# A table of steps that orders all of layer 1 instead of its first quarter

## The chip, the cores and the metric

The kernel runs on one core of one Trainium2 chip. The metric is the device time of one execution in microseconds (us), as the median of several runs. Where the text speaks of a single execution in detail, it is a profiled one: it has its own time, and a span (from its first to its last recorded instruction).

The core's engines are TensorE (PE in the profile; its weight loads are PEld), VectorE (DVE), ScalarE (ACT), GpSimd (POOL) and SyncE (SP), which here only issues transfers (DMA).

## The reference

Three computations follow each other; all numbers are float32.

```python
# 1: linear attention, 4 batches x 8 heads, 768 tokens, head_dim 32, d_state 16
L  = exp(cum[i] - cum[j]) * (i >= j)           # cum = cumsum(log a), in chunks of 32
y  = ((C @ B.T) * L) @ x  +  (C @ state) * exp(cum)
state = exp(sum(la)) * state + sum_j(B_j x_j * exp(cum_end - cum_j))
# 2: layer 1, on 3072 tokens x 256, w_gate and w_val 256 x 1536, w_out 1536 x 256
x1 = (sigmoid(y @ w_gate) * (y @ w_val)) @ w_out
# 3: layer 2, w_in 256 x 2048, w_out 2048 x 256
h  = x1 @ w_in
out = (h * sigmoid(h)) @ w_out
```

## The kernel before

**Tiling.** The kernel cuts attention into 24 chunks of 128 tokens (q = 0 to 23, six for each batch). Layer 1 works on seven blocks of tokens (b = 0 to 6), which hold 2, 2, 4, 4, 4, 4 and 4 chunks, so that a block is 256 or 512 columns wide on TensorE, and on twelve blocks of its weights (f = 0 to 11, 128 columns of w_gate and w_val and 128 rows of w_out each). Layer 2 follows with 16 weight blocks on six blocks of 512 tokens.

**Exactness.** A product of two float32 matrices is made as three products of rounded parts: each operand is split into a high part `hi` (a copy on ScalarE) and a low part `lo` (a subtraction on VectorE), and the function `three` multiplies hi by hi, hi by lo and lo by hi for both halves of 256 input features: six products for one gate tile `g`, value tile `v` or layer-2 tile `h`. Weights pass through `conv` first: ScalarE scales (line 216), VectorE makes two integer passes (218 and 220), GpSimd adds (229), ScalarE copies the high part (232), VectorE subtracts the low part (234). For token blocks 0 and 1 the output product of the first seven weight blocks uses the unsplit w_out; its split for the later blocks is a step of its own, `z`, with the subtraction in line 263.

**A chunk of attention.** Chunk q loads B and C (`b`), x (`x`) and a row of decays (`a`). VectorE's scan makes the decay matrix `L` (379). From chunk 4 on, B and C are split in three bfloat16 parts (`r`, `p`) and transposed by a DMA (`pt`). TensorE makes the scores `cb` in two halves, which share one PSUM tile; VectorE multiplies each half into `L` (429). TensorE then adds up `y` from the transposed, scaled C (`cwT`, 405) times the state (438) and from L times x (eight narrow products with 32 columns of weights, 445), and the state's increment `st` (four narrow products, 461). `yt` splits y into the operand `xT` of layer 1 (500).

**Layer 1.** For each token block and each weight block: `g` (gate, a sigmoid on ScalarE, 594), `v` (value, times the gate on VectorE, 603), `lo` (low part, 613), `o` (output, added into the tile `acc`, 634).

**What sets the order.** The string ORDER lists steps by name and index; a step is a generator, and each mention of it runs it to its next `yield`. Under `tc.manual_schedule()` every engine keeps the order of the list. In the kernel before the list ends inside token block 3's and chunk 17's steps. The rest of layer 1 comes from a loop of Python over `ticks` (one per token block and weight block). It takes the attention steps of the next token block from `slot_steps` at an even rate between the `g`, `v` and `o` of the present one. There only SyncE keeps the order of the program; on the other engines the scheduler of the language places instructions as its own estimate has them ready.

**Layer 2's weights.** They are loaded and converted during layer 1: the first four of sixteen during token block 4, the other twelve during token block 6, once the storage of attention is free (`astack.close()`), with `stg["behind"]` holding their copies behind the last output of block 5. Layer 2 itself is under the scheduler in both kernels.

Of the kernel before, what the change touches and what calls it, by code (L numbers as in the profile page):

```python
# [21 lines left out]
LAG = 2  # L22

NX = 4
# [4 lines left out]
GRP = 3  # L29
RT = 32  # L30
# [8 lines left out]
ct.2 x.3 g.0.0 v.0.0 L.3 a.4 g.0.1 w.2 cb.2.1 g.0.1 S.1 t.3 t.3 ct.2 w.2 t.3 cb.2.1 st.2 w.3 v.0.0 cb.3.0
p.4.0.2 g.0.1 bw.3 st.2 l.6 wr.3 w.3 v.0.1 l.5 w.3 y.2.0 l.4 y.2.0 y.2.1 l.4 S.2 w.3 t.3 cb.3.0 v.0.1 l.5  # L40
yt.2 w.2 v.0.1 l.4 cw.3 cb.3.1 z.0 z.1 cw.4 l.5 w.2 z.2 p.4.1.1 w.3 b.5 o.0.0 p.4.1.0 yt.2 ct.3 x.4 cb.3.1
g.0.2 ct.3 g.0.2 z.2 v.0.2 w.3 y.3.0 L.4 o.0.0 l.7 w.4 l.7 y.3.0 y.3.1 st.3 b.5 yt.3 g.0.2 pt.4.0 wr.4 w.4
bw.4 yt.3 w.4 l.6 g.1.2 v.0.2 l.6 w.3 w.4 x.6 v.0.2 w.5 g.0.3 st.3 l.7 S.3 g.0.3 r.5 g.1.2 w.5 g.1.2 g.1.0
o.0.1 w.4 g.0.3 wr.5 w.5 g.1.0 v.1.0 g.1.1 g.1.0 o.0.1 w.4 o.0.2 l.8 g.1.1 a.6 w.4 g.1.1 v.1.0 w.5 p.5.0.1
v.0.3 v.1.0 o.0.2 w.6 z.1 w.5 g.0.4 o.1.0 wr.6 v.0.3 ct.4 v.0.3 g.0.4 w.6 v.0.4 w.5 l.9 v.1.1 w.6 g.0.4 l.9
v.0.4 o.0.3 ct.4 wr.7 l.8 w.5 st.4 w.6 o.1.0 l.8 v.0.4 w.7 v.1.2 l.9 p.4.1.2 v.1.1 w.6 st.4 pt.4.1 v.1.2
v.1.1 w.7 g.1.4 o.0.3 g.1.4 cw.5 a.5 g.1.4 g.0.5 w.7 p.5.0.0 g.0.5 r.5 o.1.1 l.10 w.6 o.1.1 v.1.2 w.6 w.7
g.1.5 v.0.5 w.8 o.1.2 v.0.5 p.5.1.1 g.1.5 w.8 cb.4.0 ct.5 g.1.5 g.0.5 l.11 w.7 p.5.0.2 w.8 g.1.3 b.7 o.1.2
wr.8 o.0.4 b.6 p.5.1.2 w.7 g.1.3 p.5.1.0 w.8 v.1.3 l.10 wr.9 v.1.3 v.0.5 o.0.4 l.11 cb.4.0 g.1.3 l.10 g.0.7
w.9 v.1.3 pt.5.0 g.0.6 L.5 g.0.7 w.8 g.0.6 y.4.0 b.8 g.0.7 v.0.6 z.6 cb.4.1 b.6 o.0.5 g.0.6 ct.5 v.0.6 wr.10  # L50
w.9 v.0.7 o.1.3 pt.5.1 w.9 v.1.5 o.1.3 o.0.5 w.8 w.9 l.11 v.0.7 v.1.5 x.5 v.0.6 v.1.5 b.7 o.0.6 v.0.7 v.1.4
cb.4.1 v.0.7 v.1.4 a.7 w.10 z.6 g.0.8 r.6 v.1.4 g.1.6 w.10 g.1.6 o.0.6 r.6 p.6.1.1 lo.0.7 g.0.8 w.9 cb.5.0
v.0.8 w.10 o.1.4 g.0.8 g.1.6 v.0.8 o.1.4 p.6.1.0 w.9 wr.11 w.10 g.1.8 g.1.7 cb.5.0 g.1.8 z.4 w.11 o.0.7 o.1.5
v.0.8 g.1.7 v.0.8 v.1.6 p.6.0.0 lo.0.8 y.4.0 y.4.1 w.11 g.1.8 a.8 g.1.7 v.1.6 w.11 w.10 cb.5.1 v.1.7 o.1.5
p.6.1.2 p.6.0.2 w.11 v.1.7 pt.6.1 v.1.8 v.1.7 v.1.6 o.0.7 cb.5.1 v.1.7 v.1.8 o.1.6 lo.1.7 o.0.8 cw.7 w.11
# [24 lines left out]
v.2.11 st.13 y.12.0 v.2.10 y.12.1 a.16 cb.13.0 o.2.8 b.16 v.2.11 g.3.1 b.16 v.2.10 lo.2.11 g.3.0 yt.12  # L80
lo.2.10 p.14.0.0 o.2.9 p.14.1.0 p.14.1.2 st.13 p.14.1.1 g.3.0 pt.14.1 g.3.0 r.15 v.3.0 r.15 v.3.0 g.3.1
pt.14.0 cb.13.0 o.2.9 L.16 v.3.0 g.3.2 g.3.1 x.14 o.2.10 p.15.1.0 a.15 o.2.10 p.15.0.0 lo.3.0 v.3.1 p.15.1.1
cb.13.1 p.15.0.1 cb.13.1 g.3.2 r.16 p.15.0.2 g.3.2 o.2.11 cw.15 yt.12 pt.15.0 cw.14 L.14 o.2.11 o.2.11 g.3.3
g.3.3 cb.14.0 v.3.1 p.16.0.1 bw.14 y.13.0 o.2.11 cb.14.0 b.17 v.3.2 p.15.1.2 b.17 v.3.1 y.13.0 r.16 y.13.1
ct.14 pt.15.1 yt.13 v.3.1 v.3.2 lo.3.1 v.3.3 x.16 v.3.2 g.3.3 v.3.3 p.16.0.2 p.16.0.0 v.3.3 o.3.0 ct.14
cb.14.1 yt.13 p.16.1.1 pt.16.0 S.13 o.3.1 p.16.1.2 v.3.2 cb.14.1 r.17 o.3.0 p.16.1.0 L.15 cw.16 y.14.0 g.3.4
cb.15.0 o.3.1 y.14.0 y.14.1 r.17 st.14 st.14 x.17 lo.3.2 v.3.4 ct.15 pt.16.1 ct.15 cw.17 g.3.4 p.17.0.0 bw.15
g.3.4 cb.15.0 v.3.4 a.17 yt.14 p.17.0.1 S.14 o.3.2 x.15 yt.14 v.3.3 v.3.4 g.3.5 lo.3.3 g.3.5 p.17.1.1 v.3.4
o.3.2 p.17.1.0 lo.3.4 v.3.5 g.3.5 p.17.0.2 p.17.1.2 v.3.5
# [4 lines left out]
def tile_linattn_moe_moe(  # L94
# [115 lines left out]
    def conv(raw, hi, lo, n, whole=None):  # L210
# [20 lines left out]
        with tc.issue_after(stg["behind"]) if "behind" in stg else nullcontext():  # L231
            nc.scalar.copy(hi, f)
# [269 lines left out]
    def slot_steps(s, q0=0, q1=NQ):  # L502
        ok = lambda q: q0 <= q < q1
        st = []
        add = lambda *key: st.append(lambda: do(*key)) if ok(key[1]) else None
        early = s < 9
        if early:
            add("cb", s + 1, 0)
            add("y", s, 0)
            add("cb", s + 1, 1)  # L510
            add("y", s, 1)
        else:

            def joint():
                do("y", s, 0)
                do("y", s, 1)
                if ok(s + 1):
                    do("ct", s + 1)
                    do("st", s + 1)

            if ok(s):
                st.append(joint)
            add("cb", s + 1, 0)
            add("cb", s + 1, 1)
        add("t", s + 2)
        if ok(s + 2):
            st += [lambda: step("r", s + 2), lambda: do("L", s + 2), lambda: do("r", s + 2)]
        add("yt", s)
# [3 lines left out]
        if ok(s + 2):  # L532
            st.append(lambda: (do("bw", s + 2), do("cw", s + 2)))
# [401 lines left out]
```

## Time and profile before

| what | value |
|---|---|
| time, median of 3 runs | 652.7 us (651.78, 652.70, 654.02) |
| the profiled execution | 652.97 us, of which the span is 651.2 us |
| TensorE busy | 633.4 us, 97% of the span |
| VectorE busy | 421.3 us, 65% |
| ScalarE busy | 326.0 us, 50% |
| GpSimd busy | 111.2 us, 17% |
| chain that ended last | PE 91%, DVE 1%, ACT 1% |
| moved by DMA | 51.18 MB, mean 79 GB/s |

An engine is busy while one of its instructions executes. The chain that ended last is followed back from the last instruction to whatever released each step, so its shares say on which engine the end hangs. TensorE's granted clock was 1.00 of its full 2.4 GHz over the whole span.

### The profile page before, as it was taken

How to read it: one execution, taken by the hardware profiler on the slowest of the kernel's cores; microseconds unless marked ns; L12 is line 12 of the kernel's file. 1: busy time of each engine (PE TensorE's matmuls, PEld its weight loads, DVE VectorE, ACT ScalarE, POOL GpSimd, SP SyncE). 2: the span in 40 equal slices, each digit the busy share in tenths (PEclk: the TensorE clock that was granted, in tenths of full speed). 3: DMA queues.
4: the chain of work that ended last, by engine and by line, in shares of the span. 5: the costliest groups of instructions: out<-in, count | busy, mean ns of one | idle time of the engine just before them, and what ended most of it. 6: DMA issues, size and time to landing. Idle time of an engine off the chain costs nothing.

```text
span 651.2 us, 9850 instructions
## 1 busy us (share of the span) xinstructions
PE 633.4 (97%) x3680; PEld 518.4 (80%) x3682; DVE 421.3 (65%) x660; ACT 326.0 (50%) x649; POOL 111.2 (17%) x129
## 2 busy tenths in 40 slices
PE   4989999999999999999999999999999999999997
PEld 1468997777778877877888878888888888888886
DVE  7998898865867677574347775464655645555643
ACT  3777654453536355343255764454554544544533
POOL 4645524121203033220004310000000000000000
PEclk9999999999999999999999999999999999999999
DMA  7999757547646374341003410000000000000001
GB/s 195 243 256 238 151 106 155 116 78 170 128 99 146 74 158 117 55 144 46 0 1 97 130 34 1 1 33 0 1 34 0 18 16 1 33 1 1 33 0 34
DMA packets 140144, 51.18 MB, mean 79 GB/s; under 512 B 119008, under 2 KB 133536, under 8 KB 140096
## 3 DMA queue, kind: packets, MB, share of 16 engines
q1 hardware_dynamic: 139952, 50.41, 32.5%
q8 instruction: 29, 0.48, 0.3%
q14 instruction: 19, 0.16, 0.1%
q10 hardware_dynamic: 144, 0.13, 0.1%
HBM read 36.80 MB, written 3.24 MB: 61 GB/s over the span
## 4 chain that ended last, share of the span: by engine, by line
PE 91%; DVE 1%; ACT 1%; issue 0%; ACTq 0%
PE h L580 20%; PE acc L634 15%; PE v L580 15%; PE g L580 15%; PE o L839 13%; PE o L860 7%; PE y L445 2%; PE cb L426 2%; PE y L438 1%; PE st L461 1%; DVE w L234 0%; PE cwT L405 0%; PE o L848 0%; ACT st L361 0%; DVE cvt L220 0%
## 5 line engine op out<-in xcount | busy, mean ns | idle before, releaser
L580 PE MATMUL g<-xT,w 128*128 128x512 f32 (+1 forms) x504 | 122.3, 370 | 3.3 <-DVE xT L500 1.2
L580 PE MATMUL v<-xT,w 128*128 128x512 f32 (+1 forms) x504 | 121.2, 369 | 0.0
L580 PE MATMUL h<-x2T,w2b 128*128 128x512 f32 x432 | 107.0, 389 | 0.0
L814 DVE TENSOR_TENSOR sh<-h,sh 128x512 f32<-128x512 f32 x96 | 66.2, 691 | 61.5 <-ACT sh L813 60.0
L823 DVE TENSOR_TENSOR gl<-sh,gh 128x512 fp32r<-128x512 f32 x96 | 65.8, 690 | 57.2 <-ACT gh L818 55.8
L580 PEld LDWEIGHTS g<-xT,w 128*128 128x128 f32 x504 | 86.5, 188 | 19.7 <-DVE xT L500 1.6
L580 PEld LDWEIGHTS v<-xT,w 128*128 128x128 f32 x504 | 86.3, 189 | 14.8 <-issue 1.0
L634 PE MATMUL acc<-gh,w 128*128 128x512 f32 (+1 forms) x280 | 97.3, 382 | 0.2 <-ACT x1T L645 0.2
L580 PEld LDWEIGHTS h<-x2T,w2b 128*128 128x128 f32 x432 | 80.7, 188 | 16.5
L813 ACT ACTIVATE sh<-h 128x512 f32<-128x512 f32 x96 | 57.5, 599 | 71.3 <-PE h L580 67.3
L818 ACT CAST gh<-sh 128x512 fp32r<-128x512 f32 x96 | 59.0, 620 | 61.7 <-DVE sh L814 31.1
L572 ACT CAST gh<-sg 128x512 fp32r<-128x512 f32 (+1 forms) x70 | 41.1, 589 | 75.2 <-DVE sg L603 68.7
L603 DVE TENSOR_TENSOR sg<-v,sg 128x512 f32<-128x512 f32 (+1 forms) x84 | 50.8, 609 | 39.0 <-PE v L580 36.7
L839 PE MATMUL o<-w2b,gh 128*128 128x512 f32 x280 | 74.2, 390 | 0.0
L613 DVE TENSOR_TENSOR gl<-sg,gh 128x512 fp32r<-128x512 f32 (+1 forms) x70 | 47.8, 683 | 27.4 <-ACT gh L572 27.0
L594 ACT ACTIVATE sg<-g 128x512 f32<-128x512 f32 (+1 forms) x84 | 44.8, 537 | 34.9 <-PE g L580 30.9
L229 POOL TENSOR_TENSOR cvt<-cvt,raw 128x512 int32<-128x512 int32 (+1 forms) x28 | 44.5, 1592 | 101.8 <-DVE cvt L220 80.2
L634 PEld LDWEIGHTS acc<-gh,w 128*128 128x128 f32 x280 | 52.4, 188 | 10.4 <-ACT x1T L645 0.6
L839 PEld LDWEIGHTS o<-w2b,gh 128*128 128x128 f32 x280 | 51.8, 188 | 10.3
L379 DVE TENSOR_TENSOR_SCAN L<-L,eye 128x1024 f32<-128x1024 f32 x24 | 55.2, 2300 | 6.0 <-DMA L<-ac_d 6.0
L634 PE MATMUL acc<-gl,w 128*128 128x512 f32 (+1 forms) x140 | 52.6, 376 | 0.0
L429 DVE TENSOR_TENSOR L<-cb,L 128x512 f32<-128x512 f32 x48 | 32.7, 682 | 9.3 <-PE cb L426 7.5
(95 smaller groups left out, 730.3 us busy)
## 6 DMA issues: line engine op xcount, KB each, us to landing
L<-ac_d SPq DMA_DIRECT2D x23, 512.0 KB, 4.6
raw<-in_moe_w_out_dram SPq DMA_DIRECT2D x28, 256.0 KB, 3.3
raw<-in_moe_w_in_dram SPq DMA_DIRECT2D x16, 256.0 KB, 2.7
raw<-in_moe_w_gate_dram SPq DMA_DIRECT2D x12, 256.0 KB, 4.6
raw<-in_moe_w_val_dram SPq DMA_DIRECT2D x12, 256.0 KB, 4.8
x<-in_x_dram SPq DMA_DIRECT2D x24, 128.0 KB, 2.9
out_dram<-o2t SPq DMA_DIRECT2D x20, 128.0 KB, 1.7
bc<-in_B_dram SPq DMA_DIRECT2D x24, 64.0 KB, 3.6
```

The source lines that it names most:

```text
L379: nc.vector.tensor_tensor_scan(t["Lf"], t["Lf"], eye, 0.0, op0=ALU.mult, op1=ALU.add)
L580: nc.tensor.matmul(psum[:, :n], w[:, i, o + k * P : o + (k + 1) * P], xt[j][:, k, :n], start=(z == 0), stop=(z == len(k_terms) - 1),)
L594: nc.scalar.activation(sg[:, :n], ps[:, :n], AF.Sigmoid)
L603: nc.vector.tensor_mul(sg[:, :n], ps[:, :n], sg[:, :n])
L613: nc.vector.tensor_sub(lo[:, :n], sg[:, :n], hi[:, :n].bitcast(F32))
L634: mm = nc.tensor.matmul(o, v[:, ms], g[:, :n], start=(f == 0 and z == 0 and not (small and m)), stop=(f == NF1 - 1 and z == len(terms) - 1 ...
L813: nc.scalar.activation(sg, ps, AF.Sigmoid)
L814: nc.vector.tensor_mul(sg, ps, sg)
L818: nc.scalar.copy(hi, sg)
L823: nc.vector.tensor_sub(lo, sg, hi.bitcast(F32))
L839: nc.tensor.matmul(ps, hi[:, s], w2(f)[:, :, DM:], start=(f == 0), stop=False, skip_group_check=True,)
L860: nc.tensor.matmul(ps[:, :DM], g2[b, f][2][:, s], w2(f)[:, 0, DM:], start=False, stop=(f == NF2 - 1), skip_group_check=True,)
```

## The change

The string ORDER grows from 1015 entries to 1808 and now lists every step of layer 1, of attention and of the loading and conversion of layer 2's weights, so that all engines keep its order up to the last token block of layer 1; its first part is written anew as well. The loop over ticks, `slot_steps`, and the rule that held the conversions behind a copy are gone. Two new entries, `A` and `B`, open the two tiles for layer 2's weights, and `l2`, `w2`, `wr2` load and convert one block of them. Each engine issues the same operations on the same shapes as before; only their order differs.

```diff
-from contextlib import ExitStack, nullcontext
+from contextlib import ExitStack
...
 ORDER = """
-e.0 e.0 b.0 b.0 a.0 e.1 e.1 e.1 e.2 e.1 l.0 l.0 l.0 b.1 e.2 t.0 L.0 x.0 t.0 e.2 L.0 L.0 e.3 t.0 b.1 cb.0.0
...
+l2.15 o.6.8 v.6.9 g.6.11 lo.6.9 v.6.10 w2.13 v.6.10 g.6.11 w2.14 o.6.9 w2.14 w2.15 v.6.11 wr2.14 w2.15 o.6.9
+w2.15 wr2.15 w2.14 v.6.11 g.6.11 w2.15 w2.14 v.6.10 w2.14 w2.15 lo.6.10 v.6.11 w2.15 v.6.11
 """
...
-        with tc.issue_after(stg["behind"]) if "behind" in stg else nullcontext():
-            nc.scalar.copy(hi, f)
+        nc.scalar.copy(hi, f)
...
+    def w2_load(f):
+        return load_w(("w2", f), w2(f), f, (w2_in,), w2_out)
+
+    def w2_conv(f):
+        return conv(*pend["w2", f])
+
+    def w2_conv_r(f):
+        conv_r(pend["w2", f][0])
+
+    def open_a():
+        sstack.close()
+        w2_alloc("a", NA)
+        stg["n"], stg["raw"], stg["cvt"] = 512, 2, 2
+        stg["p"] = sstack.enter_context(tc.tile_pool(name="stg2", bufs=1))
+
+    def open_b():
+        astack.close()
+        w2_alloc("b", NF2 - NA)
+
     FN = dict(
+        A=open_a, B=open_b, l2=w2_load, w2=w2_conv, wr2=w2_conv_r,
...
-    sp_order = ExitStack()
-    sp_order.enter_context(tc.manual_schedule(engines={mybir.EngineType.SP}))
-    ends = [sum(BLOCKS[: b + 1]) for b in range(len(BLOCKS))]
...
-        run(rate)
-        do("g", b, f)
-        run(rate)
-        if prev is not None:
-            do("lo", *prev)
-        do("v", b, f)
-        prev = (b, f)
-        run(rate)
-        queue_o.append((b, f))
-        if len(queue_o) > LAG:
-            do("o", *queue_o.pop(0))
...
-    for o in queue_o[:-1]:
-        do("o", *o)
-    do("lo", *prev)
-    do("o", *queue_o[-1])
+    last = len(BLOCKS) - 1
+    do("o", last, NF1 - 2)
+    do("lo", last, NF1 - 1)
+    do("o", last, NF1 - 1)
```

Three places show how the instructions move. The first is TensorE at chunk 15, in the fourth token block (b = 3). In the rows, `g3_5` is the gate tile of token block 3 and weight block 5, `st15` the state's increment of chunk 15, `cb15_1` the second half of its scores; a number behind the last underscore tells buffers apart, and the line is that of the kernel that the row belongs to. Before:

```order
L634 MATMUL acc3_2168<-gh3_2_2190,w1_105 128x512
L634 MATMUL acc3_2168<-gl3_2_2191,w1_105 128x512
L634 MATMUL acc3_2168<-gh3_2_2190,w1_105 128x512
L461 MATMUL st15_2318<-x15_2271,bw15_2254 32x64
L580 MATMUL v3_5_2296<-xT0_3_1616,w1_105 128x512
L580 MATMUL v3_5_2296<-xT1_3_1617,w1_105 128x512
L580 MATMUL v3_5_2296<-xT0_3_1616,w1_105 128x512 x2
L580 MATMUL v3_5_2296<-xT1_3_1617,w1_105 128x512
L580 MATMUL v3_5_2296<-xT0_3_1616,w1_105 128x512
L461 MATMUL st15_2318<-x15_2271,bw15_2254 32x64 x3
```

The same place in the changed kernel:

```order
L469 MATMUL cb15_0_2306<-tr115_2122,tr015_2137 128x128
L481 MATMUL y14_2311<-cwT14_2040,S13_2120 128x128 x2
L504 MATMUL st15_2315<-x15_2233,bw15_2249 32x64 x4
L488 MATMUL y14_2311<-L14_1930,x14_2054 32x128 x8
L469 LDWEIGHTS tr015_2137
L469 MATMUL cb15_1_2338<-tr115_2122,tr015_2137 128x128
```

Before, the four products of `st15` stood apart, with a value tile between the first and the rest; now all four stand next to the eight narrow products of `y14`, and the two halves of chunk 15's scores stand directly around that group.

The second place is VectorE at the conversion of the first weights. `cvt6`, `cvt8` and `cvt13` are the conversion buffers of weight blocks 2, 3 and 4 before; `w1<-x1T` is the subtraction of step `z`; `L3` and `L4` are the decay matrices of chunks 3 and 4. Before:

```order
L263 TENSOR_TENSOR w1_105<-x1T_81,w1_105 128x256
L234 TENSOR_TENSOR w1_105<-cvt6_249,w1_105 128x512
L500 TENSOR_TENSOR xT1_1_433<-y2_406,xT0_1_432 128x2x128
L429 TENSOR_TENSOR L3_270<-cb3_1_440,L3_270 128x512
L263 TENSOR_TENSOR w1_105<-x1T_81,w1_105 128x256
L379 SCALAR_TENSOR_TENSOR L4_346<-L4_346,eye_97 128x1024
L218 TENSOR_SCALAR cvt13_485<-cvt13_485 128x768
L500 TENSOR_TENSOR xT1_1_433<-y3_478,xT0_1_432 128x2x128
L220 SCALAR_TENSOR_TENSOR cvt13_485<-raw11_409,cvt13_485 128x768
L234 TENSOR_TENSOR w1_105<-cvt8_384,w1_105 128x512
```

In the changed kernel `cvt9` and `cvt12` are the buffers of weight blocks 3 and 4:

```order
L472 TENSOR_TENSOR L3_244<-cb3_0_426,L3_244 128x512
L543 TENSOR_TENSOR xT1_1_444<-y2_407,xT0_1_443 128x2x128
L262 TENSOR_SCALAR cvt12_435<-cvt12_435 128x768
L264 SCALAR_TENSOR_TENSOR cvt12_435<-raw8_346,cvt12_435 128x768
L277 TENSOR_TENSOR w1_105<-cvt9_356,w1_105 128x512
L472 TENSOR_TENSOR L3_244<-cb3_1_468,L3_244 128x512
L422 SCALAR_TENSOR_TENSOR L4_361<-L4_361,eye_97 128x1024
L604 TENSOR_TENSOR sg0_2_479<-v0_2_454,sg0_2_479 128x256
```

The two subtractions of `z` have left this place, and weight block 3's low part (`cvt9`) now stands ahead of chunk 4's scan, where before its counterpart (`cvt8`) stood behind it.

The third place is SyncE's queue at the start. `bc0` holds chunk 0's B and C, `x1T<-in_a` is the load of `a` for the decays, `L0` its broadcast for chunk 0, `raw1` the first weight block. Before:

```order
L665 DMA x1T_81<-in_a_dram 32x768
L308 DMA bc0_117<-in_B_dram 128x8x16
L310 DMA bc0_117<-in_C_dram 128x8x16
L297 DMA L0_120<-in_a_dram 128x8x128
L673 DMA ac_d_108<-x1T_81 32x6x128
L247 DMA raw1_127<-in_moe_w_gate_dram 128x2x256
L247 DMA raw1_127<-in_moe_w_val_dram 128x2x256
```

In the changed kernel:

```order
L351 DMA bc0_115<-in_B_dram 128x8x16
L353 DMA bc0_115<-in_C_dram 128x8x16
L664 DMA x1T_81<-in_a_dram 32x768
L290 DMA raw1_120<-in_moe_w_gate_dram 128x2x256
L340 DMA L0_122<-in_a_dram 128x8x128
L290 DMA raw1_120<-in_moe_w_val_dram 128x2x256
```

B and C of chunk 0 are now ahead of `a`, the first weights ahead of chunk 0's broadcast, and the store of the clipped decays (`ac_d`) has moved behind the second weight block's first load.

## Rows read from the trace of the kernel before

**Rows 1.** Busy time by stretch: us, PE, PEld, DVE, ACT, POOL, PEclk, DMA share, GB/s.

```profile
30.00:50.00 20.00, 17.03 (x140) 13.12 (x140) 19.16 (x29) 15.05 (x35) 11.66 (x13) 1.00 0.96 253
50.00:66.00 16.00, 14.61 (x113) 13.25 (x112) 13.86 (x21) 11.55 (x23) 8.10 (x7) 1.00 0.97 237
...
100.00:320.00 220.00, 219.80 (x1382) 172.54 (x1381) 148.02 (x235) 100.59 (x211) 46.44 (x63) 1.00 0.49 108
```

**Rows 2.** Timeline of TensorE: start, us, operation, [idle before <-releaser].

```profile
38.07 0.74 PE L580 MATMUL g<-xT,w 128*128 128x256 f32 x4 [0.73 <-DVE w L234]
```

**Rows 3.** The chain that ended last, in layer 2: twelve products of 512 columns.

```profile
412.06 2.72 PE h L580 x12
```

**Rows 4.** Timeline of TensorE, a `y` group alone.

```profile
93.15 0.28 PE L634 MATMUL acc<-gl,w 128*128 128x256 f32 x1
93.27 0.28 PE L634 MATMUL acc<-gh,w 128*128 128x256 f32 x1
93.47 0.64 PE L445 MATMUL y<-L,x 128*32 128x128 f32 x16
94.05 0.62 PE L580 MATMUL g<-xT,w 128*128 128x256 f32 x3
94.51 0.40 PE L426 MATMUL cb<-tr,tr 128*128 128x128 bf16 x4
```

**Rows 5.** Timeline of TensorE, an `st` group alone.

```profile
259.94 0.39 PE L634 MATMUL acc<-gl,w 128*128 128x512 f32 x1
260.26 0.32 PE L461 MATMUL st<-x,bw 128*32 128x64 f32 x8
260.51 0.50 PE L634 MATMUL acc<-gh,w 128*128 128x512 f32 x1
260.85 1.56 PE L580 MATMUL g<-xT,w 128*128 128x512 f32 x6
```

**Rows 6.** Timeline of TensorE, both narrow groups side by side.

```profile
110.33 1.07 PE L580 MATMUL g<-xT,w 128*128 128x512 f32 x4
111.33 0.32 PE L461 MATMUL st<-x,bw 128*32 128x64 f32 x8
111.47 0.62 PE L445 MATMUL y<-L,x 128*32 128x128 f32 x16
112.02 0.38 PE L634 MATMUL acc<-gh,w 128*128 128x256 f32 x1
112.24 0.28 PE L634 MATMUL acc<-gl,w 128*128 128x256 f32 x1
```

**Rows 7.** Timeline of VectorE in the first 60 us.

```profile
11.75 0.56 DVE L218 TENSOR_SCALAR cvt<-cvt 128x768 int32<-128x768 int32 x1 [1.29 <-ACT cvt L216]
...
15.37 0.69 DVE L429 TENSOR_TENSOR L<-cb,L 128x512 f32<-128x512 f32 x1 [0.72 <-PE cb L418]
...
38.87 0.41 DVE L263 TENSOR_TENSOR w<-x1T,w 128x256 fp32r<-128x256 f32 x1
39.20 2.28 DVE L379 TENSOR_TENSOR_SCAN L<-L,eye 128x1024 f32<-128x1024 f32 x1
...
47.69 0.69 DVE L234 TENSOR_TENSOR w<-cvt,w 128x512 fp32r<-128x512 f32 x1
...
56.69 2.29 DVE L234 TENSOR_TENSOR w<-cvt,w 128x512 fp32r<-128x512 f32 x1 [0.22 <-ACT w L232]
```

**Rows 8.** Timeline of SyncE's queue, chunk 0's load of B.

```profile
1.26 0.41 SPq L308 DMA_DIRECT2D bc<-in_B_dram  x1
```

**Rows 9.** Timelines of TensorE and VectorE, the second half of a chunk's scores.

```profile
96.28 0.40 PE L426 MATMUL cb<-tr,tr 128*128 128x128 bf16 x4
96.48 0.95 PE L580 MATMUL g<-xT,w 128*128 128x256 f32 x6
...
96.71 0.69 DVE L429 TENSOR_TENSOR L<-cb,L 128x512 f32<-128x512 f32 x1 [0.43 <-PE cb L426]
```

**Rows 10.** Timeline of GpSimd.

```profile
56.57 1.85 POOL L229 TENSOR_TENSOR cvt<-cvt,raw 128x768 int32<-128x768 int32 x1
```

More of the change, by code (lines that the diff above doesn't have):

```diff
@@ L39 @@
[L39 to L43, printed above, removed]
@@ L500, in at_yT @@
         nc.vector.tensor_sub(lo, t["y"], hi.bitcast(F32))
[L502 to L528, printed above, removed]
-        if ok(s + 2) and s + 2 >= NX:
-            for i in range(2):
-                st.append(lambda i=i: ([do("p", s + 2, i, j) for j in range(3)], do("pt", s + 2, i)))
-        if ok(s + 2):
-            st.append(lambda: (do("bw", s + 2), do("cw", s + 2)))
-        if early or not ok(s):
-            add("ct", s + 1)
-            add("st", s + 1)
-        add("S", s + 1)
-        if s >= 1 and ok(s + 3):
-            st.append(lambda: (do("b", s + 3), do("x", s + 3)))
-            add("a", s + 3)
-        return st
     live = {}
@@ L564, in tile_linattn_moe_moe @@
     acc = {}
-    x1_end = []
     g1 = {}
@@ L644, in m1_out @@
                 o = a_[:, m * n : (m + 1) * n] if small else a_[:, m, :n]
-                x1_end[:] = [nc.scalar.copy(x1T[0][:, m, start_of[b] : start_of[b] + n], o)]
+                nc.scalar.copy(x1T[0][:, m, start_of[b] : start_of[b] + n], o)
     scr = lambda k, i: x1T[0][:U, k, i * S : (i + 1) * S]
-    NB0 = BLOCKS[0]
-    slots = lambda s0, s1, q0, q1: [f for s in range(s0, s1) for f in slot_steps(s, q0, q1)]
     first = scr(1, 3)
@@ L705, in tile_linattn_moe_moe @@
             step(name, *map(int, at))
-    sp_order = ExitStack()
-    sp_order.enter_context(tc.manual_schedule(engines={mybir.EngineType.SP}))
-    ends = [sum(BLOCKS[: b + 1]) for b in range(len(BLOCKS))]
-    GR = [range(g, min(g + GRP, NF1)) for g in range(0, NF1, GRP)]
-    ticks = [(b, f) for b in range(2, len(BLOCKS)) for f in range(NF1)]
-    steps = [g for s in range(ends[1], ends[2]) for g in slot_steps(s)]
-    w2st = {}
-    def run(k):
-        for _ in range(min(k, len(steps))):
-            steps.pop(0)()
@@ L720, in tile_linattn_moe_moe @@
-    NA = 4
-    w2 = lambda f: w2st["a"][:, f] if f < NA else w2st["b"][:, f - NA]
-    def w2_alloc(key, n):
-        stack, side = (ctx, "left") if key == "a" else (w1stack, "right")
-        w2p = stack.enter_context(tc.tile_pool(name=f"w2{key}", bufs=1, side=side))
-        w2st[key] = w2p.tile([P, n, 2, 2 * DM], F32R, name=f"w2{key}")
-    def w2_steps(f0, f1):
-        ld = lambda f: lambda: walk(load_w(f, w2(f), f, (w2_in,), w2_out))
-        cv = lambda f: lambda: (conv_r(pend[f][0]), walk(conv(*pend[f])))
-        st = [ld(f) for f in range(f0, min(f0 + 2, f1))]
-        for f in range(f0, f1):
-            st += [cv(f)] + ([ld(f + 2)] if f + 2 < f1 else [])
-        return st
@@ L786, in tile_linattn_moe_moe @@
-    run(len(steps))
     sstack.close()
-    sp_order.close()
     o2p = ctx.enter_context(tc.tile_pool(name="o2p", bufs=1))
```

197 lines of the change are left out of this document (107 added, 90 removed).

## The prediction

> **What bounds the kernel now.** I read the stretches first [rows 1]: one line per stretch, with what each engine was busy. From 100 to 320 us TensorE is busy 219.80 of 220.00 us, and its granted clock is 1.00 there as in the others shown, so from there on only the work that TensorE has to do counts, and how densely its products follow each other. Between 30 and 66 us it is different: TensorE is idle 20.00 - 17.03 = 2.97 us and 16.00 - 14.61 = 1.39 us, 4.36 us in all, while VectorE is busy 19.16 of 20.00 and then 13.86 of 16.00. What TensorE waits for there shows in the timeline of its instructions [rows 2]: at 38.07 us the gate product of weight block f=2 sat idle 0.73 us until VectorE had written that block's low part (line 234). So there are two regimes: a first one in which VectorE feeds TensorE, and a long one in which TensorE's own list is the time. The change moves no work between engines (every engine issues the same operations on the same shapes), so it can gain in two ways only: a shorter wait in the first regime, a denser list in the second.
>
> **The density of TensorE's list.** The full-size product of 512 columns costs 2.72 / 12 = 0.227 us [rows 3]. The group of eight products `y<-L,x` and the group of four `st<-x,bw` are narrow (128*32 in the profile). Take the stretch around one narrow group and subtract the full-size products in it. From 93.27 to 94.51 us there are one product and three of 256 columns, 0.12 us each (93.15 to 93.27), and a `y` group: 1.24 - 4 x 0.12 = 0.76 us for `y` alone [rows 4]. From 259.94 to 260.85 us there are two products of 512 columns and an `st` group: 0.91 - 2 x 0.227 = 0.46 us for `st` alone [rows 5]. From 110.33 to 112.24 us there are four of 512, one of 256 and both groups next to each other: 1.91 - 0.91 - 0.12 = 0.88 us [rows 6]. Apart they cost 1.22, together 0.88: each narrow stretch that TensorE doesn't have to enter and leave again saves 0.34 us. In the old order TensorE goes through 32 narrow stretches for chunks 4 to 23, in the new one through 22 (counted over its whole list; the shown piece at chunk 15 is one of them, and there the old order even cuts `st15` in two). Ten fewer at 0.34 is 3.4 us, and since nearly all of them lie where TensorE is never idle, I count the whole of it. Likewise the scores `cb` now follow the narrow group directly thirteen times instead of three. No row prices that alone; it is worth at least nothing, and at most 0.20 us each, the length of a score group (96.28 to 96.48) [rows 9], so 0 to 2.0; I take 0.5, near zero, because the kind of product still changes there. **Term A: -3.9 us, between -3.4 and -5.4.**
>
> **The first 66 us.** VectorE is what TensorE waits for, so I ask what leaves VectorE's row ahead of the work that TensorE needs. First the low parts of w_out for f=1 and f=2 (the `z` steps, line 263), two subtractions like the one of 0.41 us at 38.87 [rows 7]. Blocks 0 and 1 of tokens don't read them, as they use the unsplit weight; in the new order they stand behind all weight conversions. That is 0.82 us. Second, two waits: VectorE stood 1.29 us at 11.75 until the first weights were scaled, and 0.72 us at 15.37 for the second half of chunk 0's scores [rows 7]. In the new order the weights' first load is issued before the broadcast of `a`, and chunk 0's B and C come first of all, so that the transposes and score products start before VectorE's scan is over; I take both waits as gone, 2.01 us. Against it, the load of `a` for the decays now stands behind those two loads, whose issue takes 0.41 us each, by the row of the first [rows 8], and VectorE's chain starts with it: +0.82 us. The sum is -2.0 us. Bounds: it can't give back more than TensorE's idle 4.36 us of 30 to 66 us; and at the other end, the row of chunk 1's decays is now loaded behind the second weight block, and VectorE's scan of it may come later; I bound the loss by the nearest delay of VectorE that the trace shows there, 2.29 - 0.69 = 1.60 us for one subtraction [rows 7]. The transfers were busy 0.96 and 0.97 of the two stretches [rows 1]; if they set the pace there and not VectorE, the term is nothing, which lies inside these bounds. Within the stretch the subtraction of f=3's low part moves ahead of chunk 4's 2.28 us scan and others, but these follow right behind; block 1's tokens in turn come later in VectorE's row. I count that as nothing either way. **Term B: -2.0 us, between -4.4 and +1.6.**
>
> **Waits that the new order adds.** The two halves of a chunk's scores share one PSUM tile (`cb`), so the second half must wait until VectorE has multiplied the first into `L` (line 429). In the trace the half at 96.28 lets the next product start at 96.48, VectorE starts on it at 96.71 and needs 0.69 us, to 97.40: 0.92 us after TensorE could have gone on [rows 9]. In the old order full-size products stand between the halves nearly everywhere. In eight places of the new order little but a narrow stretch does, which is worth 0.88 us [rows 6] with two state products ahead of it in most. So the product is done just in time if VectorE is free at that moment. At zero wait the cost is nothing; with one more product of 0.69 us in front it is 0.69 each, 5.5 us together. Queued behind the waiting scores are the gate and value products of the token block, and through them ScalarE's sigmoid. I take 0.1 each, as 0.92 is close to what stands between. **Term C: +0.8 us, between 0 and +5.5.**
>
> **What costs nothing.** Layer 2's weights are loaded and split at other places: four of the twelve late blocks now begin in the fifth token block and the rest runs to the end of the sixth. In the old order all twelve run in the last block. From 100 to 320 us VectorE was busy 148.02 and ScalarE 100.59 of 220.00 us [rows 1], so both have room under TensorE where these steps go now, and those that leave the last block make room there. If that cover were gone, each of them would cost VectorE's two integer passes and its subtraction. SyncE's queue is ordered by the table in both kernels, and no result is written before layer 2, so a late load holds up only other loads.
>
> **The sum.** -3.9 - 2.0 + 0.8 = -5.1 us against the profiled execution's 652.97 us (span 651.2 us and 1.8 us around it): 647.9 us. That execution is 0.3 us above the median of the three runs shown, 652.7 us, so I forecast **647.6 us**.
>
> **The rivals.** (1) The first regime gives back all it can: -4.4 instead of -2.0 us, 645.2 us, and with the scores' savings at their upper end, 643.7. For it: every wait of TensorE there is for VectorE or ScalarE, not for data that never come; against it: VectorE stays busy 19.16 of 20 us. (2) The denser list is no use where VectorE is the slower engine: the attention of the last six chunks now lies wholly ahead of the fifth token block, so VectorE has more to do per token block in the fourth. If half of term A and term B are lost there, 652.7 - 2.0 - 1.0 + 0.8 = 650.5 us, and with twice term C 651.3, which can't be told from no change (0.3% of 652.7, 2.0 us, is about what a measurement of this kernel can tell). (3) The other sign: at the eight places a scan of VectorE (2.28 us each) stands in front of the product of the scores, TensorE waits about 2.0 us at each, and 16 us are lost: 647.6 - 0.8 + 16 = 663 us. It decides from 8 x 1.0 us on. For it: VectorE's row does hold a scan just ahead of chunk 12's and chunk 15's product. Against it: the scan may have started long before. (4) VectorE and GpSimd collide more often. VectorE's subtraction at 56.69 took 2.29 us where the same shape took 0.69 at 47.69, and GpSimd's addition ran from 56.57 to 58.42 [rows 7, 10]. Three more such collisions where VectorE feeds TensorE cost 3 x 1.6 = 4.8 us: 652.4 us, no change. The Trainium skill, SBUF — State Buffer, section "SBUF: two separate sides", says that a VectorE operation with two SBUF inputs and a GpSimd operation that reads SBUF lock the same port pair for a whole instruction, so that the later one stands still; by that rule any new order may collide anew, by the rows alone the collision could be an accident; the trace agrees so far, as VectorE ended 0.56 us after GpSimd.
>
> **How the numbers follow.** My forecast, 645.2 to 650.5 us, has 0.60. Rival 1 has 0.13, rival 2 0.13, rival 3 0.08, rival 4 0.06. A range of 8 in 10 leaves out the greater part of rival 3, the far end of rival 4 and a little of rival 1: 643.5 to 651.5 us. Faster by over 0.3% (below 650.7 us): the forecast, rival 1 and the better third of rivals 2 and 4, 0.79. Within 0.3%: 0.13. Slower: rival 3, 0.08.
>
> **What would show it.** Right: in 30 to 66 us VectorE's row has one such subtraction of w_out's low part (block f=0's) where it had three, and TensorE's idle there falls from 4.4 to near 2 us; at chunk 15 `st` and `y` stand in one stretch of about 0.9 us; the first product of layer 2 starts 5 us earlier. Term C shows as TensorE's idle before `cb`, released by VectorE's line that multiplies `L`. I am wrong if TensorE is idle more than 2 us in all between 100 and 320 us, or if the first regime ends no sooner than before.

## The result and the profile after

The changed kernel takes 645.14 us, the median of 4 runs (644.25 to 647.22), beside 652.93 us before (651.78 to 654.02, 4 runs): a ratio of 0.9886, 95% interval 0.9856 to 0.9915, or 7.4 us less by the ratio (7.8 by the medians). One execution each in experiments 1, 3 and 8 took about 2199 us, and the medians and ratios below leave these three out. The profiled execution took 644.25 us with a span of 642.4 us, 8.72 us less than that of before.

Everything is gained ahead of layer 2. The timelines of TensorE show its first product of layer 2 (`h`), before and after (start, duration, operation):

```profile
379.53 1.52 PE L580 MATMUL h<-x2T,w2a 128*128 128x512 f32 x6
```

```profile
370.66 2.88 PE L581 MATMUL h<-x2T,w2a 128*128 128x512 f32 x12
```

That is 8.9 us earlier, and it stays so to the end. Busy time by stretch of the new kernel, with the columns of [rows 1]:

```profile
0.00:30.00 30.00, 19.27 (x103) 9.59 (x105) 25.62 (x34) 17.68 (x45) 15.52 (x25) 1.00 0.92 217
30.00:50.00 20.00, 19.24 (x162) 16.05 (x162) 17.71 (x31) 15.69 (x36) 13.40 (x13) 1.00 1.00 242
50.00:66.00 16.00, 15.85 (x115) 14.87 (x114) 15.97 (x23) 12.15 (x24) 11.51 (x8) 1.00 0.95 244
...
100.00:320.00 220.00, 219.50 (x1397) 175.96 (x1396) 143.86 (x230) 101.72 (x210) 41.39 (x60) 1.00 0.49 105
```

Between 30 and 66 us TensorE's idle time fell from 4.36 us [rows 1] to 0.76 + 0.15 = 0.91 us. VectorE is busy 33.7 of these 36 us, as before (33.0). From 30 us to layer 2 the timeline of TensorE marks four waits:

```profile
39.16 0.39 PE L581 MATMUL g<-xT,w 128*128 128x256 f32 x1 [0.65 <-DVE w L277]
...
65.69 0.74 PE L581 MATMUL g<-xT,w 128*128 128x256 f32 x4 [0.15 <-DVE w L277]
...
224.30 0.97 PE L581 MATMUL v<-xT,w 128*128 128x512 f32 x3 [0.50 <-ACT sg L595]
...
336.30 0.50 PE L635 MATMUL acc<-gl,w 128*128 128x512 f32 x1 [0.15 <-DVE gl L614]
```

None of them stands at a score product `cb`. Chunk 15 in TensorE's timeline after, where the old order had `st` in two pieces apart from `y`:

```profile
181.48 0.40 PE L469 MATMUL cb<-tr,tr 128*128 128x128 bf16 x4
181.71 0.66 PE L481 MATMUL y<-cwT,S 128*128 128x128 f32 x4
182.30 0.32 PE L504 MATMUL st<-x,bw 128*32 128x64 f32 x8
182.44 0.62 PE L488 MATMUL y<-L,x 128*32 128x128 f32 x16
182.99 0.40 PE L469 MATMUL cb<-tr,tr 128*128 128x128 bf16 x4
183.20 0.47 PE L635 MATMUL acc<-gh,w 128*128 128x512 f32 x1
```

What attention has for TensorE there is one dense piece of 1.7 us, with `st` and the narrow `y` in one stretch, and the second `cb` follows without a wait.

**Where on the way it is gained.** The two kernels do the same products in another order, so equal times of the two traces do not show equal work. I gave every product of TensorE a fixed price by its kind (0.227 us for 512 columns, 0.119 for 256, 0.05 for one bfloat16 score, 0.0275 and 0.015 for the narrow ones, and so on, the same for all kernels), and read from each trace when the same sum was reached. The first row is the kernel before, the others are what each kernel is ahead (-) or behind (+) of it there. This is my own calculation; half a microsecond in it is a matter of which product comes first, and the first column moves by up to 3 us with the price given to the few kinds of product at the start.

```
before, us                  14.8    28.3    38.7    60.3    95.8   181.4   440.1
after                       -3.2    -0.1    -1.4    -4.9    -5.8    -7.1    -8.5
e1_first_list_before        -0.1    -0.3    -0.3    -0.4    -0.3    -0.3    -1.9
e2_first_list_after         -3.3    -0.7    -1.9    -6.3    -6.9    -7.8    -9.1
e3_conversions_before       -0.1    -0.1    -0.1    +1.1    +5.6    +4.7    +3.2
e4_st_apart                 -3.1    +1.1    -0.1    -3.9    -4.3    -3.0    -1.9
e5_before_no_add            -0.5    +0.0    -1.1    -1.0    -1.2    -1.2    -2.5
e6_after_no_add             -3.4    +0.0    -1.2    -4.7    -6.1    -7.5   -10.2
e7_before_z_late            -0.3    -0.3    -0.3    -1.0    +0.0    +0.0    -0.4
e8_start_before             -1.2    +1.5    +0.2    -4.1    -4.5    -5.8    -7.2
e9_after_f3_late            -3.0    +0.9    -0.3    +0.0    -0.6    -2.0    -3.5
e10_before_f3_early         +1.2    +1.1    +1.1    +1.0    +1.1    +1.0    +0.4
e11_after_a_first           -2.5    -0.5    -1.8    -5.1    -5.8    -6.8    -8.2
e12_before_scan4_late       -0.5    -0.7    -0.9    -0.1    +0.4    +0.6    +0.5
```

The new kernel is some 3 us ahead at first (its first product starts at 3.17 us, that of before at 6.21), has lost that by 28 us, and gains 4.8 us between 28 and 60 us. The other 3.6 us come slowly over the 320 us behind that.

### The profile page after: what moved, and what is told of

Same layout as the page of the kernel before. It is cut to its first block, busy times and chain, and to the rows that moved or that the text cites. A ratio compares the mean times of both kernels' runs of the same rounds, so it can differ in the third digit from the quotient of the medians.

```text
span 642.4 us, 9844 instructions
## 1 busy us (share of the span) xinstructions
PE 626.6 (98%) x3680; PEld 517.4 (81%) x3682; DVE 419.8 (65%) x660; ACT 327.5 (51%) x649; POOL 107.6 (17%) x129
## 4 chain that ended last, share of the span: by engine, by line
PE 86%; DVE 4%; ACT 2%; DMA 1%; issue 1%; POOL 1%; SPq 0%; ACTq 0%; DVEq 0%; POOLq 0%
PE h L581 20%; PE g L581 14%; PE acc L635 13%; PE o L785 13%; PE v L581 13%; PE o L806 7%; PE cb L469 2%; PE y L488 2%; PE y L481 1%; DMA raw<-in_moe_w_out_dram 1%; DVE cvt L264 1%; POOL cvt L273 1%; DVE cvt L262 1%; PE st L504 1%; DVE gl L614 0%
## 5 line engine op out<-in xcount | busy, mean ns | idle before, releaser
L635 PE MATMUL acc<-gh,w 128*128 128x512 f32 (+1 forms) x280 | 99.1, 380 | 0.0
L614 DVE TENSOR_TENSOR gl<-sg,gh 128x512 fp32r<-128x512 f32 (+1 forms) x70 | 49.2, 707 | 16.8 <-ACT gh L573 16.5
```

The lines of the kernel that those rows point to most:

```text
L614: nc.vector.tensor_sub(lo[:, :n], sg[:, :n], hi[:, :n].bitcast(F32))
L635: mm = nc.tensor.matmul(o, v[:, ms], g[:, :n], start=(f == 0 and z == 0 and not (small and m)), stop=(f == NF1 - 1 and z == len(terms) - 1 ...
```

## The experiments

All times are medians, with the ratio to runs of the kernel before on the same chip. The experiments ran on four chips, so a distance to the new kernel is best taken from two ratios. Single runs of one kernel lie up to 3.7 us apart, and part of that is TensorE's mean granted clock, which is between 0.992 and 1.000 in the runs listed.

**1. The old first list, the new rest.** The list holds all 1015 old entries, then the 793 entries of the new table that are left.

```diff
 ORDER = """
-b.0 e.0 b.0 e.0 l.0 a.0 l.0 l.0 t.0 e.1 b.1 ...
+e.0 e.0 b.0 b.0 a.0 e.1 e.1 e.1 e.2 e.1 l.0 ...
```

> The whole first list of the kernel before (1015 entries, to about 187 us there), then the entries of the new table that are left, in the new table's order. Theory 1 (by equal work done on TensorE, the profiled executions are 7.6 us apart at that point and 8.9 at the end): most of the gain is in the part that the old list covered, so this kernel keeps 1.3 us of it, 651.6 us. Theory 2 (the prediction's sum: 3.9 us of a denser list, spread over chunks 4 to 23, and 2.0 us in the first 66 us; nine of the twenty chunks lie behind the cut): it keeps about 1.8 us, 651.1 us. Theory 3 (the gain is in replacing the loop over ticks and the scheduler by a table): it keeps nearly all, below 647 us.

Measured: 651.78 us, ratio 0.9985 (0.9973 to 0.9996). TensorE's first product of layer 2:

```profile
377.29 2.88 PE L579 MATMUL h<-x2T,w2a 128*128 128x512 f32 x12
```

It is 2.2 us ahead of before. Replacing the loop and the scheduler by a table gives 0.8 us by the medians and 1.9 by the table above, so theory 3 falls. Theories 1 and 2 lay too close together to be told apart by this run.

**2. The new first list, the old rest.**

```diff
-l2.0 l2.0 g.3.7 p.18.0.0 a.18 v.3.7 ...
+    (the table ends here; the loop over ticks of the kernel before follows)
```

> The new table up to the entry where it holds all that the old first list holds (1044 entries), then the loop over ticks of the kernel before with the scheduler. Theory 1: 652.9 - 7.6 = 645.3 us, as good as the whole change. Theory 2: 652.9 - 4.1 = 648.8 us. Theory 3: above 651 us.

Measured: 645.59 us, ratio 0.9893 (0.9874 to 0.9912).

```profile
370.76 1.52 PE L580 MATMUL h<-x2T,w2a 128*128 128x512 f32 x6
```

The first list alone gives the whole gain. Theory 1 holds, theory 2 was 3 us off: the first list is worth more than the prediction gave it.

**3. The old list to the last conversion, the new rest.** As 1, with the cut after the last `w.11`.

> The list of the kernel before up to the last weight conversion of layer 1 (489 entries, to about 88 us there), then what is left of the new table. Theory 1 (5.1 of 8.9 us are gained by this point): it keeps 3.8 us, 649.1 us. Theory 2 (term B of the prediction, 2.0 us, was all that this stretch could give): it keeps 5.8 us of a gain of 7.8, 647.1 us.

Measured: 654.43 us, ratio 1.0024 (1.0010 to 1.0038), slower than both kernels, and a miss for both theories. Stretches of it, and TensorE's wait at the seam:

```profile
40.00:45.00 5.00, 3.44 (x38) 2.88 (x31) 4.89 (x9) 2.40 (x4) 2.44 (x3) 0.87 0.96 248
45.00:50.00 5.00, 5.00 (x31) 4.71 (x30) 3.99 (x3) 2.93 (x7) 3.61 (x4) 0.79 0.77 227
92.00:96.00 4.00, 2.67 (x15) 2.29 (x15) 2.46 (x8) 2.54 (x7) 0.95 (x2) 0.87 0.41 93
96.00:100.00 4.00, 4.00 (x39) 3.36 (x39) 4.00 (x7) 2.01 (x7) 1.17 (x2) 0.71 0.56 153
```

```profile
93.12 0.39 PE L633 MATMUL acc<-gl,w 128*128 128x256 f32 x1 [1.61 <-DVE gl L612]
```

The profiled execution was one of the longer ones, 656.06 us. Its clock fell first at 40 us, where the list is still that of before, and the table goes from -0.1 to +1.1 there. Where the two lists meet, work is left over that neither order had meant to come then: TensorE idles 1.33 of 4 us and then has a granted clock of 0.71. From there on it gains 2.4 us (+5.6 to +3.2), much as the new kernel does in the same stretch (2.7). So the run says little on the first stretch and confirms the slow gain behind it.

**4. The narrow products apart.** One entry moved at each of 13 chunks, from behind the narrow products to between them; here chunk 10:

```diff
-st.10 y.9.0 y.9.1 yt.9 a.13 cb.10.0 p.11.0.1 g.2.6
+st.10 g.2.6 y.9.0 y.9.1 yt.9 a.13 cb.10.0 p.11.0.1
```

> The new table with one full-size step of layer 1 (a half of a gate, value or output tile) moved between the state products st and the narrow products of y, for 13 of the chunks 6 to 22: 13 narrow stretches more for TensorE, nothing else. Theory A (term A of the prediction: a narrow stretch more costs 0.34 us wherever TensorE is the bound): 13 x 0.34 = 4.4 us slower than the new kernel, 649.5 us. Rival (the entry of a narrow stretch is hidden, and the rows priced something else): 645.1 us within 0.7.

Measured: 650.96 us, ratio 0.9975 (0.9965 to 0.9985), 5.8 us above the new kernel (0.0089 of 652.3 us). TensorE's busy time from 100 to 380 us:

```profile
100.00:380.00 280.00, 278.99 (x1637) 220.74 (x1636) 185.41 (x292) 135.08 (x270) 57.41 (x72) 1.00 0.44 99
```

TensorE is idle 1.01 us in 280, so it does the same products less densely. Chunk 15 in its timeline shows the price at one place:

```profile
186.35 0.32 PE L502 MATMUL st<-x,bw 128*32 128x64 f32 x8
186.60 0.50 PE L633 MATMUL acc<-gh,w 128*128 128x512 f32 x1
186.93 0.39 PE L633 MATMUL acc<-gl,w 128*128 128x512 f32 x1
187.16 0.40 PE L633 MATMUL acc<-gh,w 128*128 128x512 f32 x1
187.49 0.65 PE L486 MATMUL y<-L,x 128*32 128x128 f32 x16
188.06 0.40 PE L467 MATMUL cb<-tr,tr 128*128 128x128 bf16 x4
```

From `st` to the second scores it is 1.71 us with three full-size products in between, 1.71 - 3 x 0.227 = 1.03 us without them. In the new kernel, above, it is 182.99 - 182.30 = 0.69 us: 0.34 us more for one narrow stretch more.

The first `h` comes at 377.29 us, 6.6 us after the new kernel's; 1.5 of that is there at 95.8 us in the table already, the other 5.2 us (from -4.3 to -1.9 where the new kernel goes from -5.8 to -8.5) are 0.40 for each of the 13 stretches, and 5.8 us by the ratios are 0.45. Of the 1.5 us, 1.2 are there at 28.3 us (+1.1 beside -0.1), ahead of all moved entries, and between 25 and 30 us the granted clock of this profile was 0.69; so 0.40 is the better figure. Theory A holds, a little above its 0.34.

**5 and 6. No last addition on GpSimd,** in the kernel before and in the new one:

```diff
-        nc.gpsimd.tensor_tensor(ti, ti, r, ALU.add)
         yield
```

> The kernel before without GpSimd's last addition in the conversion of weights (line 229), so the weights lack part of their bits: 28 additions less, and with them what VectorE loses when it meets one. Theory P (VectorE and GpSimd get in each other's way, and the new order has fewer such meetings: in the first 60 us before, VectorE's instructions that overlap GpSimd's take 7.5 us more than the shortest of their kind, in the first 55 us after 4.4 us): before gains about 5 us by it, 648 us, and the distance to the new kernel without additions falls from 7.8 to about 5.5 us. Rival (the meetings cost nothing on the path): 652.9 us within 1, and the distance stays 7.8 us.

> The new kernel without the same 28 additions of GpSimd; the weights lack part of their bits. Theory P: it gains 2.5 to 3 us where before gains 5, 642.5 us. Rival: 645.1 us within 1.

Measured: 650.46 us, ratio 0.9964 (0.9951 to 0.9977), and 643.27 us, ratio 0.9862 (0.9846 to 0.9878). By the ratios that is 2.3 us less than before and 1.6 less than the new kernel, and the distance of the two goes from 7.4 to 6.7 us, a change that the intervals can't tell from nothing. But in the profile of the first TensorE's clock fell just where something was to be gained:

```profile
30.00:50.00 20.00, 18.12 (x138) 14.29 (x138) 16.44 (x29) 14.80 (x35) 6.35 (x9) 0.91 0.97 267
```

In the runs whose mean clock was 0.999 or more the medians are 649.0 (5 runs, against 652.2 us before) and 643.4 us (3 runs, against 644.6 us in 2 runs of the new kernel): 3.2 and 1.2 us, a distance of 5.6 us, near what theory P gave; these are few runs, and of two chips. By the table 1.0 us was there by 60 us in the kernel before, in a profile with that lower clock, and nothing in the new one; both gain another 1.3 us behind 181 us. The additions are thus worth somewhere between 0.7 and 2.0 us of the distance, and not the main part of the 4.9 us. What of that is meetings of VectorE and GpSimd is not shown: the addition is also a link in a weight's conversion, which is shorter without it. VectorE's instructions do stretch where they overlap GpSimd's: of the 7.64 us that they take above the shortest of their kind in the first 60 us before, 7.49 fall on such overlaps, and 4.38 of 4.51 after, up to the same work (55.4 us). This is my own count, and with another choice of what one kind is it comes out up to 0.8 us otherwise. That the stretching falls on the overlaps is as the rule in the Trainium skill, SBUF — State Buffer, section "SBUF: two separate sides", has it. That TENSOR_SCALAR, with a single input, stretches too (1.67 us beside 0.53) needs that rule's other case, which no row shows.

**7. `z` late in the old list.**

```diff
-... ct.3 g.0.2 z.2 v.0.2 w.3 ...
+... ct.3 g.0.2 v.0.2 w.3 ...   (z.1 and z.2 after the last w.11)
```

> The kernel before with one thing of the change alone: VectorE's subtractions of z for weight blocks 1 and 2 stand behind the last weight conversion. Theory 1 (VectorE feeds TensorE in the first 66 us, so what leaves its row there is gained): 0.8 us faster than before, 652.1 us. Rival (VectorE has slack at these two places, since TensorE waits for particular rows and not for VectorE's sum): 652.9 us. The difference is near what five rounds can tell.

Measured: 652.58 us, ratio 1.0003 (0.9992 to 1.0014). By the table it goes from 0.3 to 1.0 us ahead between 38.7 and 60 us and is level at 95.8. The subtractions run later, in VectorE's timeline, and TensorE then has a wait that it did not have before:

```profile
87.50 0.75 DVE L262 TENSOR_TENSOR w<-x1T,w 128x256 fp32r<-128x256 f32 x2
88.17 0.68 DVE L428 TENSOR_TENSOR L<-cb,L 128x512 f32<-128x512 f32 x1
```

```profile
89.71 0.62 PE L579 MATMUL v<-xT,w 128*128 128x256 f32 x3 [0.44 <-ACT sg L593]
```

Gained as theory 1 has it, and given back; that this wait comes from the later subtractions is likely by their place, not shown.

**8 and 11. The start.** Run 8 has the old first 62 entries, run 11 only the load of `a` first. The edit of run 11:

```diff
-b.0 e.0 b.0 e.0 l.0 a.0 ...
+e.0 e.0 b.0 b.0 l.0 a.0 ...
```

> Only the first 62 entries of the list of before (to the end of chunk 0's y, about 20 us), then what is left of the new table: the old order of the first loads and of chunk 0. Theory 1 (the new kernel is 3 us ahead at its first product but no longer at 28 us): the start is worth nothing, 645.1 us within 0.7. Theory 2 (term B counted 2.01 us for two waits of VectorE in this stretch and 0.82 against it): 1.2 us slower, 646.3 us. The other way, since VectorE's idle in the first 10 us grew from 1.62 to 4.06 us: up to 1 us faster than the new kernel, 644.1 us.

> The new table with the load of a for the decays first in SyncE's queue, ahead of chunk 0's B and C, as before the change. Term B of the prediction counted +0.82 us for its place behind them, so by it this kernel is 0.8 us faster than the new one, 644.3 us. Rival (the new kernel has lost the lead of its first products by 28 us, so nothing in the first 10 us counts): 645.1 us within 0.5.

Measured: 645.77 us, ratio 0.9899 (0.9881 to 0.9917), and 645.09 us, ratio 0.9879 (0.9862 to 0.9897). For run 8 the interval holds the new kernel's ratio, so it stays open between the theories; its profile lost time where the old start met the new list, after a stretch in which TensorE was busy 2.15 of 5 us:

```profile
15.00:20.00 5.00, 2.15 (x19) 0.97 (x20) 3.93 (x4) 4.31 (x11) 0.78 (x2) 1.00 1.11 322
20.00:25.00 5.00, 3.99 (x20) 2.02 (x19) 4.12 (x3) 1.73 (x7) 2.55 (x4) 0.66 0.97 285
```

For run 11 the rival is nearer, 645.09 us beside 645.1 and 644.3, but its interval is 1.1 us to either side and holds both. By the table it is level with the new kernel from 60 us on, so the place of that load shows no worth.

**9. One scan put back in the new table.** Chunk 4's scan ahead of block 3's low part on VectorE, and ahead of the product with chunk 3's second scores:

```diff
-cb.3.1 b.5 wr.4 w.3 b.5 p.4.0.1 o.0.1 w.4 g.0.2 cb.3.1 g.0.3 ct.3 L.4
+cb.3.1 b.5 wr.4 L.4 w.3 b.5 p.4.0.1 o.0.1 w.4 g.0.2 cb.3.1 g.0.3 ct.3
```

> The new table with one entry moved: chunk 4's scan stands ahead of the subtraction of weight block 3's low part on VectorE, as in the kernel before, instead of two places behind it. Theory V (in the kernel before VectorE's subtraction for block 3 began at 43.05 us although ScalarE's copy for it was done at 38.1, and TensorE's gate product waited for it; this was most of what the first stretch lost, and the prediction counted it as nothing): block 3's low part comes 2.3 us later and TensorE, which has little else to do there, is 1 to 2.3 us slower: 646.1 to 647.4 us. Rival D (the transfers, 0.95 to 1.00 busy up to 66 us in both kernels, set the pace of the first stretch, so VectorE's order is free): 645.1 us within 0.7.

Measured: 649.98 us, ratio 0.9949 (0.9935 to 0.9962), 4.1 us above the new kernel (0.0063 of 653.2 us), more than expected. Its wait, and the stretches there:

```profile
42.69 0.58 PE L579 MATMUL g<-xT,w 128*128 128x256 f32 x1 [3.13 <-DVE w L275]
```

```profile
40.00:45.00 5.00, 2.31 (x11) 2.32 (x12) 3.56 (x4) 0.47 (x2) 4.14 (x3) 0.75 0.59 138
45.00:50.00 5.00, 5.00 (x53) 4.47 (x53) 3.20 (x7) 3.72 (x8) 0.49 (x1) 0.91 0.34 104
...
42.60:45.90 3.30, 3.21 (x24) 2.99 (x28) 0.96 (x3) 1.37 (x3) 1.54 (x2) 0.50 0.84 243
```

TensorE stands 3.13 us for the low part, where the new kernel stood 0.65, and right behind that its granted clock is 0.50 (1.2 of 2.4 GHz) from 42.6 to 45.9 us. The wait is 2.5 us longer, and 3.21 busy us at half the clock are some 1.6 us more than at full clock (my estimate), together about the 4.1 us. By the table all of the first stretch's gain is gone at 60 us (+0.0); 1.0 us of that was gone at 28 us already, ahead of the moved entry, and the other 3.9 are the move's. Rival D falls for the new kernel: VectorE's order is what matters there.

**10 and 12. The same place in the old list.** Run 10 moves block 3's subtraction ahead of the scan, run 12 the scan behind it (and `bw.4` with it). The edit of run 10:

```diff
-w.3 y.3.0 L.4 o.0.0 ... wr.4 w.4 bw.4 yt.3 w.4 l.6 g.1.2 v.0.2 l.6 w.3 ...
+w.3 y.3.0 w.3 L.4 o.0.0 ... wr.4 w.4 bw.4 yt.3 w.4 l.6 g.1.2 v.0.2 l.6 ...
```

> The kernel before with one entry moved: the subtraction of weight block 3's low part ahead of chunk 4's scan on VectorE instead of four places behind it. Theory V: it comes 3 to 4 us earlier, TensorE's idle between 40 and 45 us (1.6 us of 5) goes, and 1.5 to 2.5 of the 4.9 us that the first stretch gains are had by this alone: 650 to 651 us. Rival D: 652.4 us within 0.6.

> The kernel before with chunk 4's scan moved on VectorE from ahead of two passes, chunk 3's operand and block 3's low part to behind them (and GpSimd's product that reads it behind block 4's additions). In the profile of before TensorE waits 0.83 us at 42.32 for chunk 3's operand and 0.37 us at 43.78 for block 3's low part, both behind that scan; moving block 3's subtraction alone gave nothing. Theory V (the place of this scan is a large part of the first stretch's gain, as it cost the new kernel 4 us when put back): both waits go, 1.2 to 2.3 us faster, 650.5 to 651.5 us. Rival W (the old list's other engines are laid out around that scan, so something else is late next, and the gain of the new list is no sum of such places): 652.6 us within 0.6.

Measured: 654.10 us, ratio 1.0010 (0.9999 to 1.0020), and 653.71 us, ratio 1.0014 (1.0003 to 1.0025). Neither gains, and run 10 lies above what either of its theories gave. TensorE's timelines, of run 10 and of run 12:

```profile
43.98 0.50 PE L579 MATMUL g<-xT,w 128*128 128x256 f32 x2 [1.42 <-DVE xT L499]
```

```profile
42.45 1.09 PE L579 MATMUL g<-xT,w 128*128 128x256 f32 x7 [0.37 <-DVE w L233]
44.02 0.62 PE L579 MATMUL g<-xT,w 128*128 128x256 f32 x3 [0.47 <-ACT sg L593]
49.45 0.38 PE L579 MATMUL g<-xT,w 128*128 128x256 f32 x1 [0.34 <-DVE w L233]
60.70 0.38 PE L425 MATMUL cb<-tr,tr 128*128 128x128 bf16 x4 [1.35 <-DMA tr<-st]
```

In run 10 the wait goes to chunk 3's operand, which is still behind the scan. In run 12 this wait is gone, and ScalarE's sigmoid, another low part and the transposed parts of chunk 4 are late in its place. Rival W is nearer: at this place of the old list one move only hands the wait on. That the other engines' order was laid out around the scan is an argument and not shown. Nor do the two runs settle rival D for the old list: one of its waits is for a transfer, 1.35 us in run 12 and 0.78 us in the kernel before:

```profile
59.53 0.38 PE L426 MATMUL cb<-tr,tr 128*128 128x128 bf16 x4 [0.78 <-DMA tr<-st]
```

## Why the prediction was right, and where its sizes were off

The forecast was 647.6 us and faster; the measured time, 645.14 us, lies inside its range. The direction and the two regimes were right. The sizes stand as follows.

**Term A, the denser list** (-3.9 us, with term C -3.1). By the table the new kernel gains 8.5 - 4.9 = 3.6 us behind the first 60 us. Experiment 4 shows the mechanism directly: 13 narrow stretches more cost 5.2 to 5.8 us, 0.40 to 0.45 each, and 0.34 at chunk 15, where [rows 4 to 6] gave 0.34. The narrow stretches are not the whole of it, though. From 95.8 to 375 us of before I count 27 of them in the trace of before and 19 after, for a gain of some 3 us; but 1.3 us of that lie ahead of 181.4 us, where the two have 9 and 8. There TensorE comes back from products of attention of any kind to full-size ones 34 times before and 18 after, and a fit to the 14 profiles of that stretch puts 0.38 us on a narrow stretch and 0.05 on a return (my estimate). So a score group or a transpose that stands alone has a price too, for which term A took 0.5 us, of the scores alone. That nearly all of it counts, because TensorE never idles there, is borne out by the 278.99 of 280 us. The first `h` was foretold 5 us earlier and came 8.9 us earlier.

**Term B, the first 66 us** (-2.0 us, at best -4.4) was mis-sized; it measured -4.9 by the table. That its sum had the right sign is luck, as none of its parts gave time in the end. The step that failed is the sentence that counted the new place of block 3's low part, ahead of chunk 4's scan, as "nothing either way". Put back in the new table it costs 4.1 us, some 2.5 of them a longer wait and the rest a lower clock behind it. Of the three sums that were counted instead none is there at the end: the `z` steps give 0.7 us and take it back (experiment 7), the later load of `a` shows no cost (experiment 11, whose interval would also allow the 0.82), and the two waits at 11.75 and 15.37 us [rows 7] did not turn into time. The lead of 3.2 us at the start is gone at 28 us, and in the first 30 us TensorE was idle 10.73 us, more than the 9.65 us of before, by this row of the kernel before:

```profile
0.00:30.00 30.00, 20.35 (x102) 9.99 (x104) 25.41 (x33) 16.89 (x44) 13.94 (x26) 1.00 0.91 219
```

Between 30 and 66 us its idle time fell by 3.45 us, to 0.91 where the prediction had near 2; the rest of the 4.9 us is no idle time, so it lies in how closely the products follow each other. VectorE's row there has one `z` subtraction instead of three, as foretold. The reason behind the term, that VectorE's order feeds TensorE, holds for the new list (experiment 9). In the old one three changes of that order moved the time by nothing or by 0.9 us the wrong way. The prediction's sentence that every wait of TensorE there is for VectorE or ScalarE does not hold for all: of 4.3 us of waits between 30 and 66 us before, 0.78 were for a transfer (the row at 59.53 us).

What remains open is a split of the 4.9 us by single moves. It is not a sum of them: taking one out loses nearly all, putting one in gains nothing. GpSimd's additions, through fewer meetings with VectorE or otherwise, are a part of 0.7 to 2.0 us.

**Term C, waits at the scores** (+0.8 us) did not come. TensorE's idle from 100 to 320 us rose by 0.3 us, from 0.20 to 0.50, at one value tile that waited for ScalarE's sigmoid, not at `cb`. Rival 3, a scan ahead of the scores' product, is not seen at any of the eight places.

**Rival 1** came nearest: the first regime gave back more than it. **Rival 2**, a VectorE too slow for the denser list, is not seen: VectorE is busy 143.86 of the 220 us, and TensorE idle 0.50. **Rival 4**, more collisions with GpSimd, went the other way, 7.5 to 4.4 us of stretched instructions.

## What to carry to other kernels

Where one engine is busy all the time, count how often its work changes between wide and narrow products; grouping the narrow ones was worth 0.34 to 0.45 us for each stretch saved, and a row with both kinds side by side is enough to see it. Where several engines feed each other, the worth of one place cannot be read off one wait: take the move out of the good order and put it into the bad one, since the two answers (4.1 us and nothing here) tell whether it acts alone. To compare two orders of the same work, read the traces at equal work, not at equal times.

## What was not expected

TensorE's granted clock can fall behind a stall of a few microseconds, but it does not always. It was 1.00 throughout in the profiles of before and after. It was 0.50 from 42.6 to 45.9 us, behind the wait of 3.13 us in experiment 9, 0.66 behind a stretch of 2.15 busy us of 5 (experiment 8), 0.66 behind one of 2.60 of 5 (experiment 9, 20 to 25 us) and 0.71 behind one of 2.67 of 4 (experiment 3). The new kernel had such a stretch as well, and no fall behind it:

```profile
20.00:25.00 5.00, 2.82 (x33) 1.54 (x35) 5.00 (x8) 3.14 (x9) 4.47 (x4) 1.00 0.96 264
```

So a wait in the first stretch can cost more than its own length. Part of the distance of single runs goes with it: in the 23 runs of before with experiments 1 to 3 and 8 the median is 652.0 us where the mean clock was 0.999 or more (14 runs) and 653.6 us where it was less (9 runs), and on the other three chips the two medians are 1.1 to 1.6 us apart in the same sense; the runs of the two groups overlap.
